# Routing attention and an ELU MLP on one core: first-batch transposes, clusters by thirds, reciprocals by Ln and Exp, masks moved behind the exponentials

## The chip, the cores and the metric

The kernel runs on one core of a Trainium2 chip. The metric is the device time of one launch in microseconds (us); smaller is better. The engines are PE (TensorE, with weight loads listed as PEld), DVE (VectorE), ACT (ScalarE), POOL (GpSimd) and SP (SyncE, which here only issues DMAs). Each works through its own instructions in order; semaphores hold an instruction until what it needs is there.

## The reference

Two blocks follow each other. The first is attention in which a query only sees keys of its own cluster; the second is an MLP with ELU over all heads of a token.

```python
# q, k, v: (4, 8, 768, 64); centroids: (8, 16, 64)
q_n, k_n, c_n = (normalised over the last axis)
q_assign = argmax(q_n . c_n)          # 16 clusters per head
k_assign = argmax(k_n . c_n)
mask   = q_assign[..., :, None] == k_assign[..., None, :]
scores = where(mask, q @ k.T / 8, -1e9)
attn   = softmax(scores)              # over keys
x      = (attn @ v) -> (3072, 512)    # tokens x (heads * 64)
h      = x @ w_in                     # (512, 2048), given as 64-bit floats
g      = where(h > 0, h, exp(min(h, 0)) - 1)
out    = g @ w_out                    # (2048, 512), given as 64-bit floats
```

## The kernel before, in words

**Blocks.** The four batches are cut into thirds of 256 queries (`QS`), and the eight heads into four pairs (`pr`). A block is one batch, third and pair; there are 48 of them, in that order. `scores(n)` makes a block's scores with keys on the partitions, in three units of 256 keys, each in two PSUM banks. For every 128 keys it adds the plain product of k and q (L406) and the mask product (L415): one-hot clusters of the keys (`hot[b, 1]`) times `qm[n]`, which holds 0 where the cluster fits and minus 2^80 elsewhere, so that the exponential (L423, ACT) gives zero there. `masks(n)` (L380, two ACT operations) makes `qm[n]` from the one-hot clusters of the queries. `values(n)` sums the exponentials times v in `o_bank` (L452), and the row sums in another bank, `d` (L441). In the first ten blocks the row sums are made by PE for each tile of keys; later DVE adds the exponentials up first (`sums`, L429 to L431), and PE makes one sum. At its end `values` copies the output and the row sums out (L466, L468, ACT), takes the reciprocal of the sums (L469, DVE) and multiplies (L470, POOL) into `xT`. `check(n)` (L476, ACT) adds the reciprocals up for a test at the end (`verdict`); if that test fails, a general path computes everything again.

**Start.** q, k, v and then the weights are loaded in order through SP's queue. For the first batch `turn` brings q and k into the layout with head dimensions on partitions: PE transposes (L322 for k; for q a product with the identity matrix for every head and tile, L326) and ACT copies (L329). Later batches are transposed by DVE (L316). `similar` forms the similarities to the centroids (L337) and transposes them with DVE (L344); `assign` takes the largest (L354), compares (L356, which also counts the hits in `count`), transposes the one-hot back (L366) and copies it to the other half of the partitions (L369). Both work in halves of 384 tokens.

**Weights.** The weights come as 64-bit floats. `weigh` advances a generator that turns one piece of 128x512 into 32-bit floats per step, pipelined over three steps: DVE L260 and L268, ACT L271 (`ex`), DVE L246, L249 and L252. There are 32 pieces. One step stands behind each exponential of the first ten blocks, and some in the MLP steps. After that `sum_weights` forms sums of parts of w_out (L301 and L303, L304 on DVE, L302 on POOL), which the MLP's second product uses: it is made from seven products (`first` to `seventh`, L521) in place of eight.

**Order.** Nothing is reordered after the program is written: each engine's order is the order of the text below. The MLP of a third follows its attention by some blocks: group n - 7 (`LAG` = 7) of the list of MLP steps stands behind block n, four groups to a third: two groups of `hidden` (L491, with its exponential L501 on ACT, L502 on POOL and L508 on DVE) and two of `outer`. Iteration n of the main loop thus is: `values(n - 1)`, loads, `masks(n + 1)`, `scores(n)` with the weight steps, `check(n - 1)`, `sums(n)`, transposes of the next batch, MLP steps; at the end of a batch the next batch's clusters stand between the MLP steps. PSUM has three double banks in turn (`banks`) for scores, row sums, similarities and hidden units, and the two banks `o_bank` and `f_bank`.

Of the kernel before, what the change touches and what calls it, by code (L numbers as in the profile page):

```python
# [9 lines left out]
F32 = mybir.dt.float32  # L10
# [8 lines left out]
P = 128  # L19
# [41 lines left out]
def main_path(ctx, tc, c, q, k, v, centroids, moe_w_in, moe_w_out, out):  # L61
# [118 lines left out]
    nc.vector.tensor_scalar(ss, ss, 1e-30, None, op0=Alu.max)  # L180

    nc.scalar.activation(r0, ss, Act.Sqrt)
    nc.vector.reciprocal(norm, r0)
    nc.vector.tensor_tensor(norm, norm, ss, op=Alu.mult)
    nc.vector.tensor_tensor(norm, norm, r0, op=Alu.add)
    nc.vector.tensor_scalar(norm, norm, 0.5, 1e-6, op0=Alu.mult, op1=Alu.add)
    nc.vector.reciprocal(norm, norm)
    nc.vector.tensor_scalar(cen, cen, norm, None, op0=Alu.mult)
    cen2 = const.tile([P, 2, D], F32, name="cen2")
    for e in range(2):  # L190
        nc.vector.tensor_scalar(cen2[:, e], cen, par[:, e : e + 1], None, op0=Alu.mult)
    cps = banks()[:, 0]
    nc.tensor.transpose(cps[:, :P], cen2.rearrange("p e d -> p (e d)"), ident)
    cT = const.tile([P, P], F32, name="cT")
    nc.vector.tensor_copy(cT, cps[:, :P])
    count = const.tile([P, 4 * B], F32, name="count")
    r_sum = const.tile([P, NQ * len(pairs)], F32, name="r_sum")
    d_sum = const.tile([P, NQ * len(pairs)], F32, name="d_sum")

# [112 lines left out]
    def turn(i, j):  # L312
        T[i, j] = turned.tile([P, S], F32, name=f"{name_of[j]}T", tag="turned")
        src = raw[name_of[j], i]
        if i >= NPR:
            nc.vector.transpose(T[i, j], src)  # L316
            return
        ps = banks()
        for t in range(NT):
            to = ps[:, t // HT, ts(t % HT, P)]  # L320
            if j == 1:
                nc.tensor.transpose(to, src[:, t].rearrange("p h d -> p (h d)"), ident)  # L322
                continue

            for e in range(2):
                nc.tensor.matmul(  # L326
                    to[64 * e : 64 * e + 64], lhsT=src[:, e, t], rhs=ident, start=True, stop=True
                )
        nc.scalar.copy(T[i, j].rearrange("p (h s) -> p h s", h=2), ps[:, :, :HS])  # L329

    def similar(b, j, half):
        if half == 0:
            sim[b, j] = route.tile([P, S], F32, name="sim", tag="sim", bufs=1)
        ps = banks()[:, 0]
        cols = slice(half * HS, (half + 1) * HS)
        for pr in range(NPR):
            nc.tensor.matmul(  # L337
                ps[32 * pr : 32 * pr + 32, :HS],
                lhsT=cT[:, 32 * pr : 32 * pr + 32],
                rhs=T[b * NPR + pr, j][:, cols],  # L340
                start=True,
                stop=True,
            )
        nc.vector.transpose(sim[b, j][:, cols], ps[:, :HS])  # L344

    def assign(b, j, half):
        if half == 0:
            hot[b, j] = route.tile([P, 2, S], BF16, name="hot", tag=f"hot{j}", bufs=1 + j)
        cols = slice(half * HS, (half + 1) * HS)
        n = HS // NC  # L350
        s = sim[b, j][:, cols].rearrange("p (n c) -> p n c", c=NC)
        top = route.tile([P, n], F32, name="top", tag="top", bufs=1)
        oh = route.tile([P, HS], BF16, name="oh", tag="oh", bufs=1)
        nc.vector.tensor_reduce(top, s, axis=Axis.X, op=Alu.max)  # L354
        at = 4 * b + 2 * j + half
        nc.vector.scalar_tensor_tensor(  # L356
            oh.rearrange("p (n c) -> p n c", c=NC),
            s,
            1.0,
            top.unsqueeze(2).to_broadcast([P, n, NC]),  # L360
            op0=Alu.mult,
            op1=Alu.is_equal,
            accum_out=count[:, at : at + 1],
        )
        h = hot[b, j]
        nc.vector.transpose(h[:, 0, cols], oh)  # L366
        for e in range(2):
            at = 64 * e
            nc.vector.tensor_copy(h[64 - at : 128 - at, 1, cols], h[at : at + 64, 0, cols])  # L369

    def side(pr, e):
        return int(pr // 2 != e)
# [18 lines left out]


    blocks = [(b, third, pr) for b in range(B) for third in range(NQ) for pr in range(NPR)]
    pu, osum, xT, rs = {}, {}, {}, {}

    def scores(n):
        b, third, pr = blocks[n]
        i = b * NPR + pr
        cols = ts(third, QS)
        for u in range(NT // 2):  # L400
            s = banks()
            for m in range(2):
                kt = 2 * u + m
                for e in range(2):
                    rows = slice(64 * e, 64 * e + 64)
                    nc.tensor.matmul(  # L406
                        s[:, e, ts(m, QS)],
                        lhsT=T[i, 1][rows, ts(kt, P)],
                        rhs=T[i, 0][rows, cols],
                        start=True,  # L410
                        stop=False,
                    )
                for e in range(2):
                    rows = slice(64 * e, 64 * e + 64)
                    nc.tensor.matmul(  # L415
                        s[:, e, ts(m, QS)],
                        lhsT=hot[b, 1][rows, side(pr, e), ts(kt, P)],
                        rhs=qm[n][rows],
                        start=False,
                        stop=True,  # L420
                    )
            p = pu[n, u] = probs.tile([P, 2, 2 * QS], F32, name="p", tag="p")
            nc.scalar.activation(p, s, Act.Exp, scale=SCALE)  # L423
            if n < LAG + 3:
                weigh(1)

# [6 lines left out]
    def values(n):  # L433

        b, third, pr = blocks[n]
        d = banks()[:, 0]
        summed = osum.pop(n, None)

        def row_sums(p, m, kt, last):
            for e in range(2):  # L440
                nc.tensor.matmul(  # L441
                    d[64 * e : 64 * e + 64, :QS],
                    lhsT=ones,
                    rhs=p[:, e, ts(m, QS)],
                    start=(kt == 0),
                    stop=(kt == last),
                )

        for kt in range(NT):
            p, m = pu[n, kt // 2], kt % 2  # L450
            for e in range(2):
                nc.tensor.matmul(  # L452
                    o_bank[64 * e : 64 * e + 64, :QS],
                    lhsT=raw["v", n][:, e, kt],
                    rhs=p[:, e, ts(m, QS)],
                    start=(kt == 0),
                    stop=(kt == NT - 1),
                )
            if summed is None:
                row_sums(p, m, kt, NT - 1)  # L460
        if summed is not None:
            row_sums(summed, 0, 0, 0)
        if pr == 0:
            xT[b, third] = xtp.tile([P, KC, QS], F32, name="xT", tag="xT")
        x = xT[b, third][:, pr]
        nc.scalar.copy(x, o_bank[:, :QS])  # L466
        r = work.tile([P, QS], F32, name="r", tag="r", bufs=1)
        nc.scalar.activation(r, d[:, :QS], Act.Copy, accum_out=d_sum[:, n : n + 1])  # L468
        nc.vector.reciprocal(r, r)  # L469
        nc.gpsimd.tensor_tensor(x, x, r, op=Alu.mult)  # L470
        rs[n] = r

    def check(n):

        r = rs.pop(n)
        nc.scalar.activation(r, r, Act.Copy, accum_out=r_sum[:, n : n + 1])  # L476


    lag = []
# [135 lines left out]
    def verdict():  # L615

        ok = c["ok"]
        peak = const.tile([P, 2], F32, name="peak")
        same = const.tile([P, 4 * B], F32, name="same")
        nc.vector.tensor_reduce(peak[:, 0:1], r_sum, axis=Axis.X, op=Alu.add)  # L620
        nc.vector.tensor_reduce(peak[:, 1:2], d_sum, axis=Axis.X, op=Alu.add)
        nc.vector.tensor_scalar(ok[:, 0:1], peak[:, 0:1], R_MAX, None, op0=Alu.is_lt)
        nc.vector.tensor_scalar(ok[:, 1:2], peak[:, 1:2], D_MAX, None, op0=Alu.is_lt)
        nc.vector.tensor_scalar(same, count, float(HS // NC), None, op0=Alu.is_equal)
        nc.vector.tensor_reduce(ok[:, 2:3], same, axis=Axis.X, op=Alu.min)
        nc.vector.tensor_reduce(ok[:, 3:4], ok[:, 0:3], axis=Axis.X, op=Alu.min)
        ps = banks()[:, 0]
# [2 lines left out]

    seen = {0}
    raw["v", 0] = raw.pop(("v", 0))
    for j in range(2):
        for pr in range(NPR):
            turn(pr, j)
        for half in range(2):
            similar(0, j, half)
            assign(0, j, half)
        if j == 0:
            masks(0)  # L640

    for n in range(len(blocks) + LAG):
        b, at = n // NB, n % NB
# [6 lines left out]
                load("k", (b + 1) * NPR + pr)  # L650
        if n + 1 < len(blocks):
            load_v(n + 1)
        if n + 1 < len(blocks) and at + 1 < NB:
            masks(n + 1)
        if n < len(blocks):
            scores(n)
        if 0 < n <= len(blocks):
            check(n - 1)
        if n < len(blocks):
            if n >= LAG + 3:  # L660
                sums(n)
# [4 lines left out]
        if ahead and at + 1 == NB:  # L666
            beside.append(None)
            for j in range(2):
                beside.append(lambda b=b, j=j: [similar(b + 1, j, half) for half in range(2)])
                beside.append(lambda b=b, j=j: [assign(b + 1, j, half) for half in range(2)])  # L670
            beside.append(lambda n=n: masks(n + 1))
        main = groups[n - LAG] if n >= LAG else []
        if n == LAG + 2:
# [272 lines left out]
```

## Time and profile before

| What | Value |
|---|---|
| Median of 3 runs | 1039.59 us (1038.36 to 1040.49) |
| Profiled execution | 1039.92 us, span of its instructions 1038.0 us |
| PE busy | 1005.5 us, 97% of the span |
| DVE busy | 515.4 us, 50% |
| ACT busy | 343.5 us, 33% |
| POOL busy | 115.4 us, 11% |
| Mean granted PE clock | 0.994 of full speed |

A row of the order of time begins with the start in us from the span's beginning and the duration, then the engine, the source line, the operation, out<-in by the program's names with partitions x elements, and the count; in square brackets stands the idle time of the engine ahead of it and what ended it. A row of busy time by stretch gives the stretch, its length, then busy time and number of instructions for each engine, the granted clock of PE, the share of time in which the DMA engines were busy, and GB/s.

### The profile page before, as it was taken

The page shows a single profiled execution, that of the slowest core. Times are in us where ns is not written, and L with a number is a line of the kernel's source. Part 1 is how long each engine was busy: PE and PEld are TensorE (multiplying, and loading weights), DVE is VectorE, ACT ScalarE, POOL GpSimd, SP SyncE. Part 2 cuts the span into 40 slices and gives each one's busy share as a digit, 9 for nine tenths or more (in the row PEclk, how much of TensorE's full clock was granted, in tenths as well). Part 3 has the DMA queues.
Part 4 walks back from the last instruction along what each step waited for, and adds up shares of the span by engine and source line. Part 5 has one row for each costly group of instructions (what it writes and reads, how often), then busy time and mean ns, then how long its engine had stood idle before and what let it go on. Part 6 is the DMA issues. An engine that isn't in the chain of part 4 may idle for free.

```text
span 1038.0 us, 14929 instructions
## 1 busy us (share of the span) xinstructions
PE 1005.5 (97%) x6403; PEld 782.5 (75%) x6403; DVE 515.4 (50%) x670; ACT 343.5 (33%) x595; POOL 115.4 (11%) x129
## 2 busy tenths in 40 slices
PE   6999989999999999999999999999999999999997
PEld 4656766777877777778778778777877887788886
DVE  4899895564343444584344236365424423433121
ACT  4676432233332332332242243234223323421010
POOL 0001121110110110111011011011011011011010
PEclk9999998999999999999999999999999999999999
DMA  9738131100122122100122112201011010000000
GB/s 281 286 119 242 59 64 28 36 16 32 36 46 46 52 41 51 51 17 16 47 47 50 36 31 51 53 26 32 16 36 31 17 36 16 31 21 1 21 0 24
DMA packets 103961, 55.60 MB, mean 54 GB/s; under 512 B 83408, under 2 KB 96720, under 8 KB 103888
## 3 DMA queue, kind: packets, MB, share of 16 engines
q1 hardware_dynamic: 103888, 54.57, 18.9%
q8 instruction: 52, 0.85, 0.3%
q14 instruction: 21, 0.17, 0.1%
HBM read 48.27 MB, written 6.29 MB: 53 GB/s over the span
## 4 chain that ended last, share of the span: by engine, by line
PE 85%; DVE 10%; ACT 3%; issue 1%; POOL 0%; DMA 0%; ACTq 0%; DVEq 0%
PE banks L491 31%; PE f_bank L521 16%; PE o_bank L521 12%; PE o_bank L452 11%; PE banks L406 9%; PE banks L441 2%; PE banks L415 2%; DVE ex L246 1%; DVE r L469 1%; DVE w_in L249 1%; ACT qm L380 1%; DVE w_in L252 1%; ACT p L423 1%; PE banks L337 1%; PE banks L326 1%; DVE ex L268 1%
## 5 line engine op out<-in xcount | busy, mean ns | idle before, releaser
L491 PE MATMUL banks<-xT,w_in 128*128 128x256 f32 x1536 | 338.4, 381 | 0.6 <-ACT p L423 0.3
L491 PEld LDWEIGHTS banks<-xT,w_in 128*128 128x128 f32 x1536 | 289.8, 190 | 48.2 <-issue 4.2
L406 PE MATMUL banks<-qT,kT 64*128 64x256 f32 x1152 | 166.1, 388 | 4.7 <-ACT p L423 4.7
L452 PE MATMUL o_bank<-p,v_raw 128*64 128x256 f32 x1152 | 143.7, 384 | 4.7 <-ACT p L423 4.7
L423 ACT ACTIVATE p<-banks 128x1024 f32<-128x1024 f32 x144 | 140.6, 1022 | 12.6 <-PE banks L415 11.0
L501 ACT ACTIVATE gT<-banks 128x1024 f32<-128x1024 f32 x48 | 49.2, 1025 | 284.8 <-PE banks L491 284.8
L469 DVE RECIPROCAL r<-r 128x256 f32<-128x256 f32 x48 | 84.0, 1750 | 119.4 <-ACT r L468 119.3
L508 DVE SCALAR_TENSOR_TENSOR gT<-gT,banks 128x1024 f32<-128x1024 f32 x48 | 58.4, 1216 | 155.3 <-POOL gT L502 155.2
L406 PEld LDWEIGHTS banks<-qT,kT 64*128 64x128 f32 x1152 | 87.6, 187 | 53.5 <-PE o_bank L452 10.4
L452 PEld LDWEIGHTS o_bank<-p,v_raw 128*64 128x64 f32 x1152 | 77.9, 137 | 57.9 <-issue 16.7
L521 PE MATMUL o_bank<-w_out,gT 128*128 128x256 f32 x384 | 91.6, 393 | 6.4 <-POOL w_out L302 6.4
L466 ACT COPY xT<-o_bank 128x256 f32<-128x256 f32 x48 | 17.7, 370 | 218.0 <-PE o_bank L452 218.0
L521 PEld LDWEIGHTS o_bank<-w_out,gT 128*128 128x128 f32 x384 | 74.1, 196 | 20.8 <-POOL w_out L302 7.5
L502 POOL TENSOR_SCALAR gT<-gT 128x1024 f32<-128x1024 f32 x48 | 51.3, 1068 | 344.7 <-ACT gT L501 344.7
L470 POOL TENSOR_TENSOR xT<-xT,r 128x256 f32<-128x256 f32 x48 | 39.7, 827 | 441.9 <-DVE r L469 441.9
L521 PE MATMUL f_bank<-w_out,gT 128*128 128x256 f32 x384 | 86.8, 379 | 0.0
L415 PE MATMUL banks<-qm,hot 64*128 64x256 bf16 x576 | 80.0, 269 | 2.0 <-DVE hot L366 2.0
L521 PEld LDWEIGHTS f_bank<-w_out,gT 128*128 128x128 f32 x384 | 73.0, 190 | 9.9
L429 DVE TENSOR_TENSOR psum<-p 128x1024 f32<-128x1024 f32 x38 | 47.0, 1236 | 42.5 <-ACT p L423 42.5
L380 ACT ACTIVATE qm<-hot,minus,big 64x256 bf16<-64x256 bf16 x96 | 56.7, 591 | 4.1 <-DVE hot L366 3.3
L430 DVE TENSOR_TENSOR psum<-psum,p 128x1024 f32<-128x1024 f32 x38 | 46.8, 1231 | 6.1 <-ACT p L423 2.7
L521 PE MATMUL f_bank<-w_sum,g_sum 128*128 128x256 f32 x192 | 44.6, 386 | 0.6 <-DVE part L568 0.6
(107 smaller groups left out, 773.5 us busy)
## 6 DMA issues: line engine op xcount, KB each, us to landing
v_raw<-in_v_dram SPq DMA_DIRECT2D x48, 384.0 KB, 3.2
w_sum<-in_moe_w_out_dram SPq DMA_DIRECT2D x12, 512.0 KB, 4.7
out_dram<-o_sb SPq DMA_DIRECT2D x24, 256.0 KB, 2.0
q_raw<-in_q_dram SPq DMA_DIRECT2D x48, 96.0 KB, 3.6
k_raw<-in_k_dram SPq DMA_DIRECT2D x48, 96.0 KB, 3.1
w_sum<-in_moe_w_in_dram SPq DMA_DIRECT2D x8, 512.0 KB, 6.8
w_out<-in_moe_w_in_dram SPq DMA_DIRECT2D x8, 512.0 KB, 10.2
w_out<-in_moe_w_out_dram SPq DMA_DIRECT2D x4, 512.0 KB, 4.3
```

Of the source, the lines that this page charges most:

```text
L380: nc.scalar.activation(qm[n][rows], hot[b, 0][rows, side(pr, e), ts(third, QS)], Act.Identity, scale=m, bias=minus[rows, pr % 2 : pr % 2 + 1],
L406: nc.tensor.matmul(s[:, e, ts(m, QS)], lhsT=T[i, 1][rows, ts(kt, P)], rhs=T[i, 0][rows, cols], start=True, stop=False,)
L415: nc.tensor.matmul(s[:, e, ts(m, QS)], lhsT=hot[b, 1][rows, side(pr, e), ts(kt, P)], rhs=qm[n][rows], start=False, stop=True,)
L423: nc.scalar.activation(p, s, Act.Exp, scale=SCALE)
L429: nc.vector.tensor_tensor(to, pu[n, 0], pu[n, 1], op=Alu.add)
L452: nc.tensor.matmul(o_bank[64 * e : 64 * e + 64, :QS], lhsT=raw["v", n][:, e, kt], rhs=p[:, e, ts(m, QS)], start=(kt == 0), stop=(kt == NT ...
L469: nc.vector.reciprocal(r, r)
L491: nc.tensor.matmul(hf[:, f], lhsT=w_in[:, ch, ts(4 * n + f, P)], rhs=xT[b, third][:, ch], start=(ch == 0 and f % 2 == 0), stop=(ch == KC - 1),
L501: nc.scalar.activation(t, hf, Act.Exp)
L502: nc.gpsimd.tensor_scalar(t, t, 1.0, 0.0, op0=Alu.min, op1=Alu.max)
L508: nc.vector.scalar_tensor_tensor(t, t, -1.0, hf, op0=Alu.add, op1=Alu.max)
L521: nc.tensor.matmul(to[:, :QS], lhsT=left[:, f], rhs=right[:, f], start=(f == 0), stop=(f == FC // 2 - 1),)
```

## The change

1. **q of the first batch.** `turn` transposes two tokens' 64 columns of one head at once (128x128, 24 transposes in all in place of 96 products of half the width). The two tokens come out on the lower and upper half of the partitions; four copies a pair bring them together, two on ACT and two on DVE.
2. **Start.** The first batch's order is: q turned, first pair of k turned, similarities of q, other pairs of k turned, clusters of q, masks. The clusters of k are made by thirds (256 tokens) within `scores(0)`: plain products of two units first, then for each unit its third's clusters, the mask products, the exponential and a weight step. The copy to the other half of the partitions is on ACT for these thirds. `count` gets one column more, and `verdict` compares two sizes.
3. **Reciprocals.** ACT takes Ln of the row sums, copies them out with their sum, copies the output with the sign changed, and takes r = exp(-ln d). DVE makes Newton's step, (d r - 2) r, which is the reciprocal with the sign changed; its sum goes to `r_sum` in the same operation, so that `check` is gone. One table set that holds both functions is loaded at the start. The copy of the row sums, `e`, shares the buffer of `sim`.
4. **Masks.** `masks(n + 1)` stands behind `scores(n)` in place of ahead of it.

```diff
     nc.scalar.activation(r0, ss, Act.Sqrt)
+    nc.scalar.preload_act_table_set("natural_log_exp_and_others")
...
         ps = banks()
-        for t in range(NT):
-            to = ps[:, t // HT, ts(t % HT, P)]
-            if j == 1:
+        if j == 1:
+            for t in range(NT):
+                to = ps[:, t // HT, ts(t % HT, P)]
                 nc.tensor.transpose(to, src[:, t].rearrange("p h d -> p (h d)"), ident)
-                continue
-            for e in range(2):
-                nc.tensor.matmul(
-                    to[64 * e : 64 * e + 64], lhsT=src[:, e, t], rhs=ident, start=True, stop=True
-                )
-        nc.scalar.copy(T[i, j].rearrange("p (h s) -> p h s", h=2), ps[:, :, :HS])
+            nc.scalar.copy(T[i, j].rearrange("p (h s) -> p h s", h=2), ps[:, :, :HS])
+            return
+        for e in range(2):
+            for t in range(HT):
+                nc.tensor.transpose(
+                    ps[:, e, ts(t, P)],
+                    src[:, e, 2 * t : 2 * t + 2].rearrange("p t d -> p (t d)"),
+                    ident,
+                )
+        for e in range(2):
+            for m in range(2):
+                to = T[i, j][64 * e : 64 * e + 64].rearrange("p (t m n) -> p t m n", m=2, n=P)
+                of = ps[64 * m : 64 * m + 64, e, :HS].rearrange("p (t n) -> p t n", n=P)
+                if e == 0:
+                    nc.scalar.copy(to[:, :, m], of)
+                else:
+                    nc.vector.tensor_copy(to[:, :, m], of)
...
+            if size == QS:
+                nc.scalar.copy(h[64 - at : 128 - at, 1, cols], h[at : at + 64, 0, cols])
+            else:
+                nc.vector.tensor_copy(h[64 - at : 128 - at, 1, cols], h[at : at + 64, 0, cols])
...
+        if n == 0:
+            turn_first = similar(0, 1, 0, QS)
+            turn_rest = similar(0, 1, QS, 2 * QS)
+            units = [banks() for _ in range(2)]
+            for u in range(2):
+                for m in range(2):
+                    plain(units[u], 2 * u + m)
+            turn_first()
+            for u in range(NT // 2):
+                assign(0, 1, u * QS, QS)
+                if u == 0:
+                    turn_rest()
+                if u == 1:
+                    units.append(banks())
+                    for m in range(2):
+                        plain(units[2], 4 + m)
+                for m in range(2):
+                    mask(units[u], 2 * u + m)
+                exponentials(units[u], u)
+                weigh(1)
+            return
...
         x = xT[b, third][:, pr]
-        nc.scalar.copy(x, o_bank[:, :QS])
         r = work.tile([P, QS], F32, name="r", tag="r", bufs=1)
-        nc.scalar.activation(r, d[:, :QS], Act.Copy, accum_out=d_sum[:, n : n + 1])
-        nc.vector.reciprocal(r, r)
+        e = route.tile([P, QS], F32, name="e", tag="sim", bufs=1)
+        nc.scalar.activation(r, d[:, :QS], Act.Ln)
+        nc.scalar.activation(e, d[:, :QS], Act.Copy, accum_out=d_sum[:, n : n + 1])
+        nc.scalar.activation(x, o_bank[:, :QS], Act.Copy, scale=-1.0)
+        nc.scalar.activation(r, r, Act.Exp, scale=-1.0)
+        nc.vector.tensor_tensor(e, e, r, op=Alu.mult)
+        nc.vector.scalar_tensor_tensor(
+            r, e, -2.0, r, op0=Alu.add, op1=Alu.mult, accum_out=r_sum[:, n : n + 1]
+        )
         nc.gpsimd.tensor_tensor(x, x, r, op=Alu.mult)
-        rs[n] = r
-    def check(n):
-        r = rs.pop(n)
-        nc.scalar.activation(r, r, Act.Copy, accum_out=r_sum[:, n : n + 1])
...
-    for j in range(2):
-        for pr in range(NPR):
-            turn(pr, j)
-        for half in range(2):
-            similar(0, j, half)
-            assign(0, j, half)
-        if j == 0:
-            masks(0)
+    for pr in range(NPR):
+        turn(pr, 0)
+    turn(0, 1)
+    for half in range(2):
+        similar(0, 0, half * HS, HS)()
+    for pr in range(1, NPR):
+        turn(pr, 1)
+    for half in range(2):
+        assign(0, 0, half * HS, HS)
+    masks(0)
...
+        if n < len(blocks):
+            scores(n)
         if n + 1 < len(blocks) and at + 1 < NB:
             masks(n + 1)
-        if n < len(blocks):
-            scores(n)
-        if 0 < n <= len(blocks):
-            check(n - 1)
```

## The prediction

> **What bounds the kernel now.** I read the page first (engine totals, slices), then busy time by stretch with cuts at block borders, then the order of time inside one block of each stage, the chain of waits, and the DMA issues with their landing.
>
> From the page:
>
> ```profile
> PE 1005.5 (97%) x6403; PEld 782.5 (75%) x6403; DVE 515.4 (50%) x670; ACT 343.5 (33%) x595; POOL 115.4 (11%) x129
> ...
> PE   6999989999999999999999999999999999999997
> ...
> DVE  4899895564343444584344236365424423433121
> ```
>
> PE leaves only some 33 us idle, so nothing that helps another engine can bring much more than that. DVE is full only in slices 2 to 6, the weight conversion. Busy time by stretch:
>
> ```profile
> core 0: us, PE busy (x) PEld busy (x) DVE busy (x) ACT busy (x) POOL busy (x), PEclk, DMA share, GB/s
> 64.20:74.10 9.90, 8.98 (x86) 5.68 (x84) 9.80 (x17) 7.10 (x15) 1.05 (x1) 1.00 0.42 134
> ...
> 94.00:116.80 22.80, 22.80 (x150) 17.86 (x148) 19.98 (x32) 10.91 (x20) 4.22 (x3) 1.00 0.40 136
> 116.80:140.60 23.80, 23.09 (x150) 17.86 (x148) 22.84 (x34) 11.29 (x19) 3.33 (x3) 1.00 0.39 94
> 140.60:168.50 27.90, 21.48 (x104) 16.62 (x102) 24.26 (x24) 6.49 (x13) 7.74 (x3) 0.82 0.22 43
> ```
>
> Blocks 1 to 6 repeat every 9.93 us with DVE full and PE at 9.0: DVE sets the pace. From 94 to 116.8 PE is full. From 140.6 the weight sums on DVE and POOL hold PE up for 6.4 us (its waits for POOL's w_out L302, 4.52 and 1.89). After 168 PE is over 99% busy. One turn of the DVE-bound stage, in order of time:
>
> ```profile
> 65.71 1.74 DVE L469 RECIPROCAL r<-r 128x256 f32<-128x256 f32 x1
> ...
> 67.37 0.62 DVE L246 SCALAR_TENSOR_TENSOR ex<-w_out,ex 128x512 uint32<-128x512 uint32 x1
> ...
> 71.19 1.00 ACT L423 ACTIVATE p<-banks 128x1024 f32<-128x1024 f32 x1
> ...
> 72.25 0.65 PE L452 MATMUL o_bank<-p,v_raw 128*64 128x256 f32 x4 [0.92 <-ACT p L423]
> ...
> 73.16 0.72 ACT L271 ACTIVATE ex<-ex,off 128x512 uint32<-128x512 uint32 x1 [0.97 <-DVE ex L268]
> ...
> 73.79 0.40 ACT L476 ACTIVATE r<-r 128x256 f32<-128x256 f32 x1
> ...
> 74.12 0.70 PE L406 MATMUL banks<-qT,kT 64*128 64x256 f32 x4
> ```
>
> Call S the time DVE starts L246 behind the reciprocal (67.37). ACT's third `ex` waits for a DVE step and starts at S+5.79; ACT is free at S+6.42; PE ends the block's values at S+6.75.
>
> In the steady stage nine blocks (three begin a batch) lose time in their third unit of scores, which waits for the first exponential to free a bank:
>
> ```profile
> 294.74 0.37 ACT L466 COPY xT<-o_bank 128x256 f32<-128x256 f32 x1 [1.73 <-PE o_bank L452]
> ...
> 295.23 0.38 ACT L468 ACTIVATE r<-banks 128x256 f32<-128x256 f32 x1
> ...
> 295.60 1.20 ACT L380 ACTIVATE qm<-hot,minus,big 64x256 bf16<-64x256 bf16 x2
> ...
> 296.82 1.94 ACT L423 ACTIVATE p<-banks 128x1024 f32<-128x1024 f32 x2
> ...
> 297.90 0.70 PE L406 MATMUL banks<-qT,kT 64*128 64x256 f32 x4 [0.40 <-ACT p L423]
> ```
>
> **Part 1, the reciprocal.** DVE loses 1.66 us per block (65.71 to 67.37) and gains a product and a fused operation on 256 columns. The nearest rows are DVE's other 128x256 operations (L558, L574: 0.42) and an accumulator read (0.08). The second needs the first's result, so 0.45 + 0.47 = 0.92: DVE has 0.74 less. [...]
>
> ACT loses copy, copy with sum, and check; it gains Ln, copy with sum, scaled copy, exponential. Spacings in the trace: 0.26 for a copy of 256 columns, 0.37 with the sum, 0.41 to the end of one from SBUF (L476). Ln has no row; it takes a copy's 0.28, at most a whole 0.40. Chain from Ln to the end of Exp: 0.28 + 0.37 + 0.26 + 0.41 = 1.32, at most 0.40 + 0.58 + 0.40 + 0.42 = 1.80 if nothing overlaps. Before, copy to end of sum took 0.73 (64.25 to 64.98). No table switch is due: the changed program has two table loads in all, both at the start. x and r both change sign; POOL's product is as before.
>
> **Part 2, masks behind the exponentials.** 1.2 us of ACT leave the place ahead of a block's first exponential and stand behind its third `ex`. In blocks 1 to 6 that is a new queue: Ln for the block's sums stands behind masks, masks behind `ex`, `ex` behind DVE. So: `ex` free at S+6.42, masks to S+7.63 (PE was done at S+6.75), Ln to Exp 1.32, handover 0.04, DVE 0.92: next S at S+9.91. Before: 9.93. DVE's work alone would allow 8.27 + 0.92 = 9.2, and PE 9.0; the wait that replaces the reciprocal is ACT's. Six turns: -0.1 us.
>
> In the steady stage ACT has time behind the exponentials (next work 2 to 6 us later), so masks cost nothing there. Ahead of the first exponential: Ln can't start before the row sums (295.23), then 0.28 + 0.37 + 0.26 + 0.31 = 1.22, so 296.45 instead of 296.82: 0.37 earlier. Room for it: the third unit starts at 297.90 and PE could at 297.33. At a batch's start the tile `e` shares the buffer of `sim`, whose last reader (L356) ends at 215.78, after the row sums (215.31): 0.25 there. Six times 0.37 and three times 0.25: -3.0 us. Bounds 0 and the whole loss, -5.8 (six times 0.57, three times 0.8 or so). The o_bank is freed 0.9 later, but its next matmul is 3.4 us off.
>
> **Part 3, the start.** q: 24 transposes of 128 columns replace 96 half-width matmuls; L322's six of that size took 0.87. The copies go to ACT and DVE, four of 384 columns a pair, about 1 us on each. q's last pair lands at 9.5, so qT is ready near 12.1 (before 14.6). But k's last piece, issued at 11.88, lands 5.1 later at 17.0: kT at 18.75, similarities of the first third 19.7, of the rest (512 columns) 21.4, plain scores of two units 23.1 on PE, while DVE ends q's clusters at 19.9 and the first third of k at 21.6. First exponential near 23.7 (before 26.61), second 25.9 (28.93), third 28.8 (30.61, the last third's chain on DVE and ACT). The values start at 28.8 instead of 29.91: -1.1. A second stop is near: block 1's values need v, which another issue brings:
>
> ```profile
> 27.24 0.38 SPq L120 DMA_DIRECT2D v_raw<-in_v_dram  x1
> ```
>
> It lands 10.2 later, at 37.4; block 1's values would start at 37.6 (before 38.70). SP's queue is unchanged in order, and DMA is at 1.0 of its time until then, so no more than 1.3 us can come from the start. Bounds: -1.3, and +1.5 if ACT's two copies a third take the 0.59 of a mask and DVE is held by the q copies.
>
> **Part 4, the weight sums.** Block 7's reciprocal waits for ACT before and after: +0.1. Block 8's (143.37) is backlogged: -0.74. PE waits 0.6 less at 161.48. Block 8's scores also lose 0.7 of PE waiting, but PE then waits longer for the same sums. **Part 5:** the verdict has one DVE operation more, and PE waits for it: +0.15.
>
> Sum: -1.1 - 0.1 - 0.6 - 3.0 + 0.15 = -4.65. The profiled execution took 1039.92 (span 1038.0 and 1.9 around it), 0.33 over the median 1039.59; from the median, **1034.9**.
>
> **Rivals.** *The saved DVE time pays in full* (ACT is free in time, because `ex` comes earlier than I have it): turns of DVE's 9.2, 6 x 0.73 = 4.4 in place of 0.1: 1030.6. For it: DVE is 99% busy, and ACT only 72%. Against: the order of ACT's queue. Chance 0.25.
>
> *Hardly anything:* the start gains nothing and the first exponential is no earlier; -0.6 + 0.15: 1039.1, no change. Chance 0.12.
>
> *Slower, by a longer chain:* ACT's four operations end at 1.80 instead of 1.32. This chain stands in 16 places (start, six turns, nine steady blocks); +0.48 each is +7.7: 1042.6. It decides from 0.29 per chain. For it: Ln and Exp have no rows at this size; against: ACT's like operations do overlap. Chance 0.08.
>
> *Slower, by table loads between Ln and Exp.* The load row is 1.28 us here (L423, once). Two a block in six turns and nine steady blocks: 15 x 2.56 = 38, near 1073. [...] Chance 0.03.
>
> **How the numbers follow.** My forecast has 0.52; with the first rival, 0.77 for faster by over 0.2% (2.1 us, about what a measurement of this kernel can tell), 0.12 within, 0.11 slower. The range runs from a little under the first rival, 1029.5 (its turns at PE's 9.0), to the second, 1039.2; the slower cases are left out.
>
> **What would show it.** Right: DVE idle about 0.7 us a block before the product, released by ACT, blocks 1 to 6 still 9.8 to 10 us apart, masks between the third `ex` and Ln; first exponential near 23.7, block 1's values at 37.5; steady third units waiting 0.1 or less; two table loads. Wrong: turns near 9.2 (first rival), exponentials of the steady stage later than before (third), or `r_sum` failing its test, after which the general path would run as well.

## The result and the profile after

The changed kernel takes **1039.76 us** (median; 1038.80 to 1040.34) beside 1040.04 (1038.36 to 1040.81) for the kernel before: a ratio of 0.9999, with an interval of 0.9981 to 1.0016. That is no change, where 1034.9 was forecast. Both profiled spans are 1038.0 us. So the question is where 4.65 us of expected gain went.

The page after, engine totals and slices of PE, DVE and the granted clock:

```profile
PE 1008.0 (97%) x6331; PEld 781.2 (75%) x6331; DVE 478.0 (46%) x775; ACT 350.9 (34%) x605; POOL 112.2 (11%) x129
...
PE   6999989999999999999999999999999999999997
...
DVE  7689895463333334474234236365324423432121
...
PEclk9999997999999999999999999999999999999999
```

DVE's total fell by 37.4 us (515.4 before): 48 divisions of 1.75 us became 48 pairs of 0.425 each, with an accumulator read of 0.08. PE has 2.5 us more. Nothing that the change saved on DVE is in the time. The order of time in one turn of the DVE-bound stage, from the DVE operation `L249` that follows a block's Newton step to the next such one (columns: start, duration, engine, line, operation, and in brackets the idle time before it with its releaser):

```profile
67.25 0.69 DVE L249 SCALAR_TENSOR_TENSOR ex<-w_out,ex 128x512 uint32<-128x512 uint32 x1
...
73.13 0.72 ACT L274 ACTIVATE ex<-ex,off 128x512 uint32<-128x512 uint32 x1 [0.97 <-DVE ex L271]
...
73.76 1.20 ACT L401 ACTIVATE qm<-hot,minus,big 64x256 bf16<-64x256 bf16 x2
74.09 0.70 PE L425 MATMUL banks<-qT,kT 64*128 64x256 f32 x4
...
74.98 0.38 ACT L524 ACTIVATE r<-banks 128x256 f32<-128x256 f32 x1
75.27 0.38 ACT L525 ACTIVATE e<-banks 128x256 f32<-128x256 f32 x1
...
75.77 0.36 ACT L526 ACTIVATE xT<-o_bank 128x256 f32<-128x256 f32 x1
76.03 0.41 ACT L527 ACTIVATE r<-r 128x256 f32<-128x256 f32 x1
76.47 0.43 DVE L528 TENSOR_TENSOR e<-e,r 128x256 f32<-128x256 f32 x1 [0.77 <-ACT r L527]
77.00 0.42 DVE L529 SCALAR_TENSOR_TENSOR r<-e,r 128x256 f32<-128x256 f32 x1
77.35 0.69 DVE L249 SCALAR_TENSOR_TENSOR ex<-w_out,ex 128x512 uint32<-128x512 uint32 x1
```

A turn is 77.35 - 67.25 = 10.10 us, against 9.94 before. PE ends the block's values at 74.09 and goes on to the next scores, but ACT doesn't look at the sums until 74.98: the masks (`L401`) stand in its queue ahead of the logarithm (`L524`), behind an `ex` (`L274`) that waited 0.97 for DVE. DVE then stands idle for 0.77, released by ACT's exponential (`L527`).

Busy time by stretch (us; busy time and instructions of each engine; PEclk is the granted clock). The first row is the start of block 0's values, the second the time around the end of the weight sums:

```profile
27.59:31.00 3.41, 3.41 (x17) 1.95 (x18) 1.88 (x4) 2.88 (x5) 0.00 (x0) 0.50 1.02 408
153.90:167.60 13.70, 9.98 (x23) 7.47 (x24) 11.06 (x7) 0.37 (x1) 5.15 (x2) 0.50 0.23 36
```

In both PE runs at half its clock. The same view of the kernel before shows the second stretch shorter (last row), and its row for 24 to 35 us has a clock of 1.00:

```profile
24.00:35.00 11.00, 9.01 (x84) 5.56 (x80) 8.64 (x22) 4.99 (x7) 0.00 (x0) 1.00 1.03 410
...
154.50:164.80 10.30, 7.10 (x16) 5.21 (x17) 10.23 (x7) 0.00 (x0) 4.63 (x2) 0.50 0.30 47
```

What that costs is in the chain of waits after, behind POOL's part of the sums: the first product into f_bank takes 4.70 us instead of 3.45, and the next begins at 178.66 instead of 177.33, though the step before both began 0.08 earlier than in the kernel before (161.48). First the kernel before, then the changed one:

```profile
161.48 3.61 PE o_bank L521 x8
165.09 3.45 PE f_bank L521 x16
177.33 3.65 PE f_bank L521 x16
...
161.40 3.78 PE o_bank L577 x8
165.18 4.70 PE f_bank L577 x16
178.66 3.65 PE f_bank L577 x16
```

### The profile page after: what moved, and what is told of

Read it like the earlier page. It is cut to its first block, busy times and chain, and to the rows that moved or that the text cites. A ratio compares the mean times of both kernels' runs of the same rounds, so it can differ in the third digit from the quotient of the medians.

```text
span 1038.0 us, 15007 instructions
## 1 busy us (share of the span) xinstructions
PE 1008.0 (97%) x6331; PEld 781.2 (75%) x6331; DVE 478.0 (46%) x775; ACT 350.9 (34%) x605; POOL 112.2 (11%) x129
## 4 chain that ended last, share of the span: by engine, by line
PE 84%; DVE 10%; ACT 4%; issue 1%; POOL 0%; DMA 0%; DVEq 0%; ACTq 0%
PE banks L547 31%; PE f_bank L577 16%; PE o_bank L577 12%; PE o_bank L506 10%; PE banks L425 9%; PE banks L495 2%; PE banks L437 2%; DVE ex L249 1%; ACT p L448 1%; DVE w_in L252 1%; DVE w_out L252 1%; PE banks L353 1%; DVE w_in L255 1%; ACT e L525 1%; DVE ex L271 1%
## 5 line engine op out<-in xcount | busy, mean ns | idle before, releaser
L448 ACT ACTIVATE p<-banks 128x1024 f32<-128x1024 f32 x144 | 144.6, 1019 | 6.2 <-PE banks L437 4.2
L524 ACT ACTIVATE r<-banks 128x256 f32<-128x256 f32 x48 | 18.4, 383 | 235.0 <-PE banks L495 234.9
L528 DVE TENSOR_TENSOR e<-e,r 128x256 f32<-128x256 f32 x48 | 20.4, 425 | 161.0 <-ACT r L527 160.8
L401 ACT ACTIVATE qm<-hot,minus,big 64x256 bf16<-64x256 bf16 x96 | 56.6, 590 | 1.1
```

The costliest lines, as they stand in the source:

```text
L401: nc.scalar.activation(qm[n][rows], hot[b, 0][rows, side(pr, e), ts(third, QS)], Act.Identity, scale=m, bias=minus[rows, pr % 2 : pr % 2 + 1],
```

## The experiments

Every kernel was timed beside the kernel before, 5 times or more; ratios are to that kernel on the same chip. There were three chips, on which the kernel before took 1040.31 (e1 to e4), 1040.71 (e5 to e8) and 1039.68 (e9), so a difference of medians across them can be off by 1 us. By the ratios, e1 is 5.1 us faster than the changed kernel, e5 4.3, e6 7.9 and e9 8.6; the text has the differences of the medians. "Turn" is the length of a block in the DVE-bound stage, read as above.

| kernel | edit | us | ratio (95%) | turn, us |
|---|---|---|---|---|
| e1_masks_mid | masks between two exponentials in blocks 1 to 9 | 1034.92 | 0.9950 (0.9936 to 0.9963) | 9.24 |
| e2_masks_ahead | masks ahead of the scores everywhere | 1049.65 | 1.0090 (1.0076 to 1.0104) | 9.24 |
| e3_old_reciprocals | DVE's reciprocal back | 1039.58 | 0.9994 (0.9985 to 1.0003) | 10.50 |
| e4_old_start | start of before | 1040.58 | 1.0001 (0.9992 to 1.0010) | 10.09 |
| e5_pe_kept_busy | matmuls in PE's idle times | 1036.14 | 0.9958 (0.9944 to 0.9971) | 10.09 |
| e6_mid_and_busy | e1 and e5 | 1032.14 | 0.9923 (0.9909 to 0.9936) | 9.24 |
| e7_mid_busy_deferred | e6, reciprocal's chain spread | 1034.37 | 0.9941 (0.9927 to 0.9955) | 9.24 |
| e8_old_recip_mid | e3, masks as in e1 | 1036.41 | 0.9963 (0.9949 to 0.9977) | 9.94 |
| e9_new_then_old_recip | e6, DVE's reciprocal from block 10 | 1030.75 | 0.9916 (0.9903 to 0.9930) | 9.24 |

**Where the masks stand.** The theory: in the turns it is their place in ACT's queue, not the length of the reciprocal's chain, that eats DVE's gain. e1 moves them in blocks 1 to 9 from behind the last exponential to behind the second, where ACT waits for DVE anyhow:

```diff
             exponentials(s, u)
+            if u == 1 and n < LAG + 3:
+                masks(n + 1)
...
-        if n + 1 < len(blocks) and at + 1 < NB:
+        if n + 1 < len(blocks) and at + 1 < NB and not 0 < n < LAG + 3:
             masks(n + 1)
```

> The changed kernel, with masks(n + 1) of blocks 1 to 9 placed behind the block's second exponential, where ACT waits 1.75 us for DVE anyway; later blocks as in the changed kernel. Theory (ACT's queue: the third ex, then masks, then Ln sets the turn of blocks 1 to 6, 10.09 us with DVE idle 0.77 in each): the turn falls to DVE's own work, 8.36 + 0.88 = 9.2, six turns save 5: about 1034.7. Rival (the new chain of four ACT operations and two DVE operations is itself too long, wherever the masks stand): turns stay at 9.9 or more, at most 1 us saved, 1038.8.

Measured: 1034.92. A turn in the order of time:

```profile
65.26 0.69 DVE L249 SCALAR_TENSOR_TENSOR ex<-w_out,ex 128x512 uint32<-128x512 uint32 x1
65.77 1.01 ACT L448 ACTIVATE p<-banks 128x1024 f32<-128x1024 f32 x1
...
66.68 1.20 ACT L401 ACTIVATE qm<-hot,minus,big 64x256 bf16<-64x256 bf16 x2
...
68.52 0.72 ACT L274 ACTIVATE ex<-ex,off 128x512 uint32<-128x512 uint32 x1 [0.64 <-DVE ex L271]
...
72.26 0.38 ACT L526 ACTIVATE r<-banks 128x256 f32<-128x256 f32 x1 [0.42 <-PE banks L497]
...
73.62 0.42 DVE L530 TENSOR_TENSOR e<-e,r 128x256 f32<-128x256 f32 x1
...
74.50 0.69 DVE L249 SCALAR_TENSOR_TENSOR ex<-w_out,ex 128x512 uint32<-128x512 uint32 x1
```

The logarithm (here `L526`) now waits for PE's sums, not for masks, and the product (`L530`) starts with no idle time on DVE ahead of it. The `ex` behind the masks still waits 0.64 for DVE, so the masks delay nothing. 74.50 - 65.26 = 9.24: DVE's own work. The theory holds: six turns save 6 x 0.85 = 5.1, where it named 5. The whole time has more in it than the masks, since the half clock fell otherwise too. It lasted about 6.8 us in block 0 (worked out from the granted clock of 0.69 from 24 to 35 us) and about 3.4 twice around the weight sums (0.50 from 151.2 to 154.6, 0.51 from 158.0 to 161.5), where the changed kernel has 3.41 and 13.65: block 0's `L249` came 0.55 later (37.56), and from the half product behind POOL's sums to the second product into f_bank it took 15.93 (157.30 to 173.23) instead of 17.26. A comparison at full clock stands below (e5 and e6).

e2 puts the masks ahead of the scores in every block, as in the kernel before, and leaves the new reciprocals:

```diff
+        if n + 1 < len(blocks) and at + 1 < NB:
+            masks(n + 1)
         if n < len(blocks):
             scores(n)
-        if n + 1 < len(blocks) and at + 1 < NB:
-            masks(n + 1)
```

> The changed kernel with masks(n + 1) ahead of scores(n) again in all blocks; the new reciprocals and the new start stay. Theory: turns of blocks 1 to 6 near 9.2 (5 us saved), but in nine steady blocks the first exponential comes 1.2 later and with it the third unit of scores: +11, so 1045.7, slower than both. Rival (the masks' place matters little, the reciprocals' chain is what counts): within 1 us of the changed kernel, 1039.8.

Measured: 1049.65, slower than expected. The turns were 9.24 here too, but the steady stage paid. PE's waits there, from 180 to 940 us (us in total, times, longest), in the kernel before and in e2, and a third unit of e2 in the order of time:

```profile
PE banks L406 <- ACT p L423: 4.3, 9, 0.8
...
PE banks L425 <- ACT p L448: 12.3, 9, 1.4
...
297.81 0.70 PE L425 MATMUL banks<-qT,kT 64*128 64x256 f32 x4 [1.37 <-ACT p L448]
```

Each of nine blocks waits 1.4 us, 12.3 in all, where the kernel before waited 4.3. With Ln, copy, copy and Exp ahead of it, the first exponential can't also have the masks ahead of it. So the move of the masks is needed by the reciprocals in the steady stage, and harmful to them in the turns.

**The reciprocals alone.** e3 undoes that part and keeps the others; the check on the reciprocals is an ACT operation again, behind the masks:

```diff
-        e = route.tile([P, QS], F32, name="e", tag="sim", bufs=1)
-        nc.scalar.activation(r, d[:, :QS], Act.Ln)
-        nc.scalar.activation(e, d[:, :QS], Act.Copy, accum_out=d_sum[:, n : n + 1])
-        nc.scalar.activation(x, o_bank[:, :QS], Act.Copy, scale=-1.0)
-        nc.scalar.activation(r, r, Act.Exp, scale=-1.0)
...
+        nc.scalar.copy(x, o_bank[:, :QS])
+        nc.scalar.activation(r, d[:, :QS], Act.Copy, accum_out=d_sum[:, n : n + 1])
+        nc.vector.reciprocal(r, r)
```

> The changed kernel with DVE's reciprocal, the two copies and check() again; masks stay behind the exponentials (check behind them), the start stays new. Theory (in blocks 1 to 6 ACT's queue and not DVE sets the turn, so the reciprocal's 0.74 us of DVE buys little there, and in the steady stage the shorter chain of two copies lets the first exponential start when its scores are ready): turns 10.5 (+2.5 us in six), no wait of the third unit in steady blocks (-4.2), block 8's reciprocal +0.7: 1038.8, not slower than the changed kernel. Rival (the reciprocals pay their DVE time): turns of 10.8, about 1044.

Measured: 1039.58, the same as with the new ones. Turns took 10.50, as expected: the masks hold up the old chain as well, and the check stands behind them too. But in the steady stage PE's matmuls have no wait at all for an exponential. ACT's rows in e3 of the block that the prediction shows of the kernel before:

```profile
296.78 0.38 ACT L524 ACTIVATE r<-banks 128x256 f32<-128x256 f32 x1
...
298.00 2.11 ACT L448 ACTIVATE p<-banks 128x1024 f32<-128x1024 f32 x2 [0.74 <-PE banks L437]
```

ACT is ready 0.74 before PE has the scores. In the changed kernel the same exponential follows ACT's chain without a gap (shown further down).

**2 x 2 of the turns.** e8 is e3's edit with e1's place for the masks (both diffs above).

> e3_old_reciprocals with masks(n + 1) of blocks 1 to 9 behind the second exponential as in e1_masks_mid. Theory (with ACT's queue out of the way DVE's work sets the turn, and only then do the reciprocals count): turns of 9.94 as in the kernel before, against 9.24 with the new reciprocals and 10.50 with masks behind; 6 x 0.56 = 3.4 less than e3_old_reciprocals: 1036.2. Rival (the old reciprocals' turn is held by their own chain): turns stay at 10.5, 1039.6.

Measured: 1036.41, turns 9.94.

| turn, us | masks ahead of the scores | masks between exponentials | masks behind the block |
|---|---|---|---|
| DVE's reciprocal | 9.94 (before) | 9.94 (e8) | 10.50 (e3) |
| Ln, Exp, Newton | 9.24 (e2) | 9.24 (e1) | 10.09 (the change) |

The new reciprocals are worth 0.70 a turn, as the forecast's DVE sum had it (0.74), wherever the masks are out of the way. Behind the block the masks cost 0.56 or 0.85.

**The start.** e4 is the kernel before with the new reciprocals and masks behind, so the change without its new start; its diff is that of the change, less what stands there for the start.

> The kernel before with the new reciprocals and the masks behind the exponentials, so the changed kernel without its new start. Theory (the start brings block 0's values 2.3 us forward, but PE then runs them at a granted clock of 0.5, which takes 1.7 back): first Newton step 0.6 later than in the changed kernel, clock 1.0 from 24 to 35 us, 1040.4. Rival (the start keeps its 2.3): 1042.

Measured: 1040.58, beside 1039.76 of the whole change: 0.8 us (0.2 by the ratios), which two intervals of 0.1% and 0.2% can't tell from nothing. The trace shows why it is so little. The granted clock between 24 and 35 us is 1.00 in e4 and 0.84 in the changed kernel:

```profile
24.00:35.00 11.00, 8.68 (x60) 4.84 (x62) 4.60 (x12) 6.47 (x12) 0.00 (x0) 0.84 1.03 409
...
24.00:35.00 11.00, 9.01 (x82) 5.58 (x82) 8.41 (x21) 5.37 (x7) 0.00 (x0) 1.00 1.03 406
```

(the first row the changed kernel, the second e4). The values of block 0 begin 2.3 us earlier than before, and lose most of it in the 3.41 us at half clock.

**The clock.** e5 puts small products of the identity with itself, which nothing reads, into PE's idle times: eight in block 0, and 16 ahead of each half of the product that waits for the weight sums.

```diff
+    def fill(to, times):
+        for _ in range(times):
+            nc.tensor.matmul(to[:, :P], lhsT=ident, rhs=ident, start=True, stop=True)
...
         for f in range(FC // 2):
+            if idle is not None and f % (FC // 4) == 0:
+                fill(idle, 16)
```

> The changed kernel with matmuls on the identity matrix, whose results nothing reads, in PE's idle times: eight between the masks of block 0 (into f_bank), and twice sixteen ahead of the two halves of the product that waits for POOL's weight sums (into a free bank), all shorter than the wait that they stand in. Theory (PE's waits of 3 to 4 us are followed by a granted clock of 0.5, which costs the changed kernel 1.7 us in block 0's values and 3.3 us behind the weight sums): clock 1.0 throughout, block 0's first Newton step 1.5 earlier, product and values behind the sums 3.3 shorter, 1035. Rival (the clock row doesn't tell of lost time, PE waits for something else there): no gain, or the matmuls' own time on top, 1040 to 1043.

Measured: 1036.14, 3.6 us less than the changed kernel. Both stretches are at full clock:

```profile
24.00:35.00 11.00, 10.09 (x90) 6.67 (x91) 5.12 (x13) 7.94 (x16) 0.00 (x0) 1.00 1.02 409
140.00:162.00 22.00, 21.09 (x146) 18.22 (x142) 21.73 (x24) 5.75 (x12) 7.79 (x3) 1.00 0.29 54
162.00:180.00 18.00, 17.49 (x123) 13.22 (x124) 7.71 (x13) 5.78 (x11) 0.72 (x1) 1.00 0.08 23
```

Block 0's Newton step came 1.5 us earlier (34.7 instead of 36.2), and from the half product behind POOL's sums to the second product into f_bank it took 15.1 (159.96 to 175.02) instead of 17.3 (161.40 to 178.66). That second gain is 2.2 where 3.3 was expected; 0.56 of the rest is a new wait of the first product into f_bank, at 162.51, for DVE's `o_sb` (L623), which stands behind DVE's part of the weight sums.

**Together, and one step further.** e6 is e1 with e5.

> e1_masks_mid with the same matmuls in PE's idle times. Theory: the turn of 9.24 stays, 1.4 at the start and 2 behind the weight sums come on top: 1031.5. Rival (DVE's full queue hides the clock's cost at the start, and the sums set the end anyway): 1034 to 1035.

Measured: 1032.14. The two gains nearly add up: 4.8 and 3.6 make 8.5 (before rounding), and 7.6 of the 1039.76 were measured. Part of what is missing shows in the trace: block 1's values wait 0.74 for the landing of v, the second stop that the prediction names, and e6's first turn takes 9.60. With the clock at 1.00 in both kernels and on one chip, e5 and e6 differ by the place of the masks alone: 4.0 us. e7 then tries to save the steady stage's third units by spreading the chain over the next block's exponentials:

```diff
+        if LAG + 3 <= n + 1 < len(blocks):
+            later.extend([out_copy, newton])
...
             exponentials(s, u)
+            if u != 1 and later:
+                later.pop(0)()
```

> e6_mid_and_busy, and from block 10 on the copy of the output stands behind the next block's first exponential, and Exp, Newton's step and the product behind its third. Theory (in nine steady blocks the first exponential waits for four ACT operations, of which only Ln and the copy of the sums must come first, since they free a bank): first exponential 0.57 earlier there, of which the third unit of scores can use 0.3: 9 x 0.3 = 2.4 to 2.7 less than e6_mid_and_busy, 1029. Rival (the third unit waits for the bank of the row sums, not for the exponential): no change against e6_mid_and_busy.

Measured: 1034.37, slower than e6 by 2.2. The third units gained only some 0.1 each, and a new wait came at two batch starts (the same view of waits):

```profile
PE f_bank L601 <- DVE o_sb L654: 1.9, 2, 0.9
```

e6 has no such wait. The product on POOL comes later, and beside it DVE's sums of a block's exponentials took 1.63 instead of 1.23. Whether the later product causes the slower sums was not tried.

e9 is e6 with the kernel before's copies, reciprocal and check from block 10 on, where DVE has time; blocks 0 to 9 keep the new chain:

```diff
+        if n < LAG + 3:
             nc.scalar.activation(r, d[:, :QS], Act.Ln)
...
+        else:
+            nc.scalar.copy(x, o_bank[:, :QS])
+            nc.scalar.activation(r, d[:, :QS], Act.Copy, accum_out=d_sum[:, n : n + 1])
+            nc.vector.reciprocal(r, r)
```

> e6_mid_and_busy with the new reciprocals for blocks 0 to 9 alone; from block 10 on the copies, DVE's reciprocal and check() of the kernel before, behind masks that stand behind the exponentials. Theory (where DVE is full the new reciprocals pay, where PE is full only the time ahead of the first exponential counts, and there two copies of 0.73 us beat four operations of 1.35; e3_old_reciprocals needs 241.4 us a batch there, e6_mid_and_busy 242.3): turns stay at 9.24, about 1 us less in each of three batches: 1029. Rival (a bank or DVE gives it back, as in e7_mid_busy_deferred): 1032 or more.

Measured: 1030.75, the best of all, 0.8% under both kernels of the case. It is 1.4 below e6, but on a chip where the kernel before was 1.0 faster as well: 0.7 by the ratios, with intervals that overlap. The trace supports a gain. From the second product into f_bank behind the sums to the same product of the last third it takes 788.24 us (171.41 to 959.65) instead of 790.91, since a third of a batch (from a product into f_bank to the same one a third later) takes 79.41 instead of 79.53, and the passage to the next batch 82.62 instead of 83.26. Those are e3's lengths too, and neither e3 nor e9 has the changed kernel's 0.27 waits for the copy into `e`.

## Why the prediction was wrong

The parts, on the traces of before and after:

| step of the sum | forecast, us | measured, us |
|---|---|---|
| start | -1.1 | -0.5 |
| six turns | -0.1 | +0.85 |
| weight sums | -0.6 | -0.4 |
| clock behind the weight sums | not in the sum | +1.4 |
| steady stage | -3.0 | -1.4 |
| verdict at the end | +0.15 | +0.05 |
| sum | -4.65 | 0.0 |

The measured terms are how far the changed kernel's start times lead or lag those of before, each step against the one above it: block 0's `L249` (37.01 and 37.54, 0.5 ahead); the end of block 6's Newton step or reciprocal (97.5 and 97.2, 0.3 behind); the half product that waits for the weight sums (161.40 and 161.48, 0.1 ahead); the f_bank product (178.66 and 177.33, 1.3 behind); a product near the end of the steady stage (957.50 and 957.55, level). Of the 4.65 that are missing, the steady stage has 1.6, the clock 1.4, the turns 0.95 and the start 0.6.

**What was right.** The mechanism of the turns: DVE idle 0.77, released by ACT; masks between the third `ex` and Ln; no gain from the reciprocal there. The first rival, DVE's saving paid in full, did not happen in this kernel, and the reason given against it, the order of ACT's queue, is shown by e1, which gives it its 9.24. DVE's pair of operations cost 0.88 (76.47 to 77.35) where 0.92 was said, so the nearest rows were right: the product took 0.43, the fused operation 0.42. There is no table load between Ln and Exp (the trace has two, of 1.28 us each, at 0.75 and 3.58), and the general path did not run.

**The steady stage ("Six times 0.37 and three times 0.25: -3.0 us")** is the largest step that failed: it gave -1.4. The rows of the same block in the changed kernel:

```profile
296.41 0.38 ACT L524 ACTIVATE r<-banks 128x256 f32<-128x256 f32 x1 [2.22 <-PE banks L495]
...
296.69 0.38 ACT L525 ACTIVATE e<-banks 128x256 f32<-128x256 f32 x1
297.08 0.20 ACT L525 ACTIVATION_READ_ACCUMULATOR e<-banks 128x1 f32 x1
297.19 0.37 ACT L526 ACTIVATE xT<-o_bank 128x256 f32<-128x256 f32 x1
297.45 0.41 ACT L527 ACTIVATE r<-r 128x256 f32<-128x256 f32 x1
297.76 1.99 ACT L448 ACTIVATE p<-banks 128x1024 f32<-128x1024 f32 x2
```

The working had 0.28 + 0.37 + 0.26 + 0.31 = 1.22; it is 0.28 + 0.50 + 0.26 + 0.31 = 1.35. The copy with the sum holds ACT 0.50 rather than 0.37, since its accumulator is read 0.39 after its start (0.28 in this block of the kernel before). So a block gains 0.26, not 0.37: a third takes 79.53 instead of 79.79, six times. That is 0.7 of the 1.6 that the stage is short.

The other 0.9 is at the batch starts, where the copy into `e` also waits for the last reader of `sim`. The working took 0.12 off the gain for that wait, and read the kernel before at one start of three. At the second, before and after:

```profile
457.30 0.60 PE L441 MATMUL banks<-psum,ones 128*64 128x256 f32 x4
...
458.01 0.38 ACT L468 ACTIVATE r<-banks 128x256 f32<-128x256 f32 x1
...
458.51 1.19 ACT L380 ACTIVATE qm<-hot,minus,big 64x256 bf16<-64x256 bf16 x2
...
459.73 1.94 ACT L423 ACTIVATE p<-banks 128x1024 f32<-128x1024 f32 x2
...
457.98 0.60 PE L495 MATMUL banks<-psum,ones 128*64 128x256 f32 x4
...
459.48 0.38 ACT L525 ACTIVATE e<-banks 128x256 f32<-128x256 f32 x1 [0.42 <-DVE oh L374]
...
460.13 0.70 PE L425 MATMUL banks<-qT,kT 64*128 64x256 f32 x4 [0.27 <-ACT e L525]
...
460.56 1.99 ACT L448 ACTIVATE p<-banks 128x1024 f32<-128x1024 f32 x2
```

From PE's row sums (`L441`, `L495`) to the first exponential the changed kernel takes 2.58 at each of the three starts. The kernel before took 2.72 at the first, which the working read: there its copy of the sums began 1.00 behind the row sums (214.31 to 215.31). At the other two it began 0.7 behind, and the exponential followed after 2.43 and 2.42. So the three starts changed the time by -0.14, +0.15 and +0.14, not by three times -0.25. The kernel before also shows the long copy with the sum, at these starts: 0.50 from 458.01 to 458.51. PE's wait of 0.27 with the second unit, for the bank of the row sums, is not the cause: in the chain of waits the third unit (461.62) follows the first exponential.

What the masks' move alone is worth there, e3 shows: without the new chain it starts that f_bank product at 179.69, 2.36 behind the kernel before, and the one near the end at 955.84, 1.71 ahead of it. That is 4.1, of which the chain of four on ACT, with its wait at the batch starts, takes 2.7 back. In the turns the new reciprocals give 6 x 0.41 = 2.5. So e3 and the changed kernel have the same median within 0.2: the new reciprocals were worth about nothing in this order.

**The turns** ("so: `ex` free at S+6.42, masks to S+7.63, ... next S at S+9.91") were short by 0.19. With S at 67.25, the third `ex` started at S+5.88 instead of 5.79, Ln at S+7.73 instead of 7.63. Then Ln to the end of Exp took 1.46 instead of 1.32, 0.13 of it the copy with the sum again, and the Newton step's two operations 0.88. Six turns of 0.15 over the 9.94 of before make the +0.85.

**The clock** had no term. The prediction shows a granted clock of 0.82 from 140.6 to 168.5 in the kernel before, and puts no price on a change of it. By the trace's record of the clock the stretch at half clock around the end of the sums became 13.65 us from 10.24, which cost 1.4 though the sums were ready no later; e5 removes it, and the half clock of before with it. At the start the first exponential was earlier than forecast (22.50, with 23.7 forecast and 26.61 before), but then came 3.41 us at 0.50, in which four value matmuls take 1.12 and 1.07 instead of 0.60, and so about 1.7 of the 2.3 that the values started earlier. In the kernel before PE was busy for 0.15 us of the 3.42 ahead of the drop at 154.55; in the changed kernel for 0.92 of the 3.41 ahead of the drop at 153.91. The stretches at half clock that end within the two spans last 3.41, 10.24 and 13.65 us, one, three and four times 3.41. In steps of 3.41 us from the drop, PE was busy for 63, 48 and 97% of the time in the kernel before, and for 47, 64, 81 and 100% in the changed one, whose drop came 0.64 earlier. The third step before and the third after:

```profile
161.37:164.79 3.42, 3.31 (x8) 2.68 (x9) 3.42 (x4) 0.00 (x0) 0.06 (x1) 0.50 0.00 0
...
160.74:164.15 3.41, 2.75 (x7) 2.21 (x8) 3.41 (x4) 0.00 (x0) 0.61 (x1) 0.50 0.00 0
```

In the changed kernel the wait for the sums reached 0.66 us into this step (until 161.40), and a fourth step at half clock followed; in the kernel before it reached 0.11 into it (until 161.48), and the next step was at 1.00. What decides between the two was not shown. The half clock also differs between executions of one kernel: over 21 executions of the kernel before on the chip of e1 to e4 the mean granted clock goes from 0.992 in the slowest (1041.64) to 0.998 in the fastest (1037.61). All four of the changed kernel have 0.991 or 0.992. So the 1.4 is that of the two profiled executions; that the changed kernel has more half clock is not theirs alone.

At the start no wait of PE ahead of the drop at 27.59 was over 1.1 us, where e5's theory has waits of 3 to 4 us, but PE was busy for only 1.64 of the 4.59 us from 23.00 to 27.59.

The second rival (hardly anything, 1039.1) came nearest in time, by another way than it gave: the start and the first exponentials did gain, and longer turns and the clock took it back. The third, ACT's chain at over 0.29 more, was right in kind and not in size: the chain grew by 0.13 or 0.14.

## What to carry to other kernels

Work on an engine whose queue is in order cost here what stood behind it, not what it took (the masks' 1.2 us of ACT: nothing between two exponentials, 0.85 a turn behind the block): put it where that engine waits anyhow (the masks between two exponentials: 4.0 us for that move alone, from e5 to e6), and cost a stage's chain with its own accumulators and releases. A faster way to the same result was worth having here only where its engine is the bound (0.70 us a turn where DVE is full, e8 to e1; in the steady stage a third of a batch takes 79.53 with it and 79.41 without, e6 and e9): the best kernel has the new reciprocals in the ten blocks where DVE is full, and the old ones after them. And waits of PE had a second price here, a clock at 0.50 for 3.41 us at the start and 13.65 us around the weight sums, and filling them was worth 3.6 us (e5): look at the granted clock of each stretch where PE waits, and try to fill it if nothing better is there.

## What was not expected of the hardware

- **Filling PE's waits made the kernel faster:** 3.6 us of 1039.76 for matmuls that nothing reads, by holding the granted clock at 1.00 (e5), and 7.6 together with the masks' move (e6).
- **The half clock lasted 3.41, 10.24 and 13.65 us,** one, three and four times 3.41, and it came also after a stretch with many short waits rather than one long one (in the changed kernel at 27.59, with PE 36% busy over the 4.59 us ahead of it).
- **A copy with a sum** held ACT for 0.50 us in the changed kernel, in the turns and in the steady stage; for 0.37 in most blocks of the kernel before, but for 0.50 at its batch starts; for 0.35 in e1's turns (72.54 to 72.89), but for 0.50 in e1's steady stage, with the same size, source and queue. The accumulator is read 0.39 after the copy's start in the one case, 0.26 in the other. The cause stays open.
- **Ln of 128 x 256 from PSUM** takes the 0.38 of a copy (0.28 to the next operation), and follows and precedes Exp without a load of tables.
